# First loads of the query and key weights in row parts, two more homes for residual tiles, and a new instruction order in a fused adaLN attention and MLP block

## The chip, the cores and the metric

The kernel runs on one core of a Trainium2 chip. The metric is the device time of one execution in microseconds (us). Before the change three runs took 323.55, 323.23 and 323.64 us, a median of 323.55 us. A difference of 0.2% of that is 0.65 us.

## What is computed

One transformer block with adaptive layer norm, on 2048 tokens of width D = 640, all in bfloat16. The reference, cut to what matters:

```python
mod = (silu(c) @ w_mod)                      # 6 vectors of 640
sa, ca, ga, sb, cb, gb = mod                 # shift, scale, gate, twice
h = layernorm(x) * (1 + ca) + sa
q, k, v = split(h @ wqkv)                    # 32 heads of 20
scores = q @ k.T * 20 ** -0.5                # key j is seen by query i where 0 <= i - j < 256
x = x + ga * ((softmax(scores) @ v) @ wo)
h = layernorm(x) * (1 + cb) + sb
x = x + gb * ((sigmoid(h @ w_gate) * (h @ w_up)) @ w_down)   # hidden width 1536
```

## The kernel before

The tokens go through in 8 chunks of 256, two blocks of 128 each. A chunk `a` passes these stages: layer norm (`ln1`), the projections to Q, K and V (`qkv`), attention in two halves of 16 heads (`attention`), output projection and residual add (`outproj`), second layer norm, and the MLP (`mlp`). In attention the keys of one half are done in score sets, five a half (two for the first chunk, in three pieces): a set is a group of small matmuls into the one PSUM tile S, ScalarE (ACT) takes the exponentials of it into a tile E (line 1019), GpSimd (POOL) masks E (line 1044), and after the last set TensorE (PE) multiplies E with V in one burst. Because there is one S, PE cannot begin a set before ACT has read the set ahead of it.

The program is not run in the order in which it is written. Every operation is recorded in a list with its engines, a duration and its dependencies. `Prog.schedule` then walks the operations in the order of a table of numbers, `PRIO`: each entry gives an operation its rank (number divided by 5) and its engine (the remainder: 0 PE, 1 ACT, 2 VectorE = DVE, 3 POOL, 4 SyncE = SP). The scheduler also keeps a clock of estimates, with which the table was searched; the emitted program holds only the order, the choice of engine, the choice of buffers in each pool, and the semaphore waits. Each engine takes its instructions strictly in that order, so an instruction that waits holds up all that stands behind it on its engine. That holds for SP and ACT, which issue the DMAs, too.

What the change touches:

- `load_w3` (before: line 638) loads a column range of `wqkv` (640 x 1920, held as 128 partitions x 5 row tiles x 1920). Q's and K's columns come in four pieces of 320 columns, 400 KB each; V's in one piece of 800 KB. `R_w3` holds the resource that a projection waits for, one for each 160 columns.
- `qkv` (line 912) multiplies the normalized chunk `hT` with five row tiles of `wqkv`, a chain of five matmuls into one PSUM bank. For the first chunk a chain is 320 columns wide, later 480.
- `p_x1`, the pool of tiles that hold the residual x: 6 homes. The first three chunks' x stays in it from the start (`KEEP` = 3); later chunks load x again in `outproj` (line 1136), and that load waits for the stores of the chunk three earlier, which frees the home (`stored.get(a - 3)`).
- `load_x` (line 613), the loads of x, with estimates of how late they land.
- `mod_rows` makes two of the modulation vectors on PE from parts of `w_mod`, which lie for a time in the room of `wu` and of `hh`; matmuls written `M<-wu,silubc` and `M<-hh,silubc` are these.

Of the kernel before, what the change touches and what calls it, by code (L numbers as in the profile page):

```python
# [13 lines left out]
D = 640  # L14
# [3 lines left out]
NDT = D // 128  # L18
# [63 lines left out]
class Prog:  # L82
# [70 lines left out]
    def schedule(self):  # L153
# [37 lines left out]
        for o in sorted(self.ops, key=lambda x: x.prio):  # L191
# [41 lines left out]
            if o.isdma:  # L233
# [6 lines left out]
                o.end = max((own if e == "act" and own < bw else bw) - 0.83, st + dur)  # L240
                s = rr
# [120 lines left out]
def c_pe(n):  # L362
# [122 lines left out]
KEEP = 3  # L485
# [25 lines left out]
def build(nc, A_x, A_wqkv, A_wo, B_x, B_w_gate, B_w_up, B_w_down, c, w_mod, out, S=2048):  # L511
# [61 lines left out]
    def R(name):  # L573
        return Res(name)
# [716 lines left out]
```

## Time and profile before

| | |
|---|---|
| median of three runs | 323.55 us (323.23 to 323.64) |
| the profiled execution's own time | 324.34 us |
| its span, first to last instruction | 322.6 us |
| granted TensorE clock | 1.000 |
| PE busy | 316.8 us (98%), 4877 matmuls |
| ACT busy | 218.0 us (68%) |
| DVE busy | 207.1 us (64%) |
| POOL busy | 177.0 us (55%) |

A row of the profile names the line, the engine, the operation, the tile that is written and the tiles that are read, and the shape. Rows in order of time begin with the start and the length in us; what stands in brackets is the idle time of the engine ahead of the row and what ended it. PEld is the loading of weights into TensorE, which overlaps the matmuls. The chain that ended last is followed back from the last instruction, at each step to what released it. Matmuls are pipelined, so the length of a row of many matmuls reaches a little into the next row; the distance from start to start is the time that a row costs.

### The profile page before, as it was taken

To read this page: it belongs to the slowest core of one execution; us is meant where nothing else is said; L and a number is where in the kernel's file an instruction comes from. 1 tells how busy PE (TensorE), PEld (TensorE's weight loads), DVE (VectorE), ACT (ScalarE), POOL (GpSimd) and SP (SyncE) were. 2 spreads that over 40 slices of the span, in tenths; PEclk is the share of its full clock that TensorE was granted. 3 is DMA by queue.
4 is the path that set the end of the run, shared out by engine and by line. 5 is a ranking of instruction groups with operands and counts; after the bars stand their busy time and mean duration, and the time that the engine had idled before them with its cause. 6 is when DMAs were issued, how large, how long until landed. Compare 5 with 4: busy or idle time off the path is not lost.

```text
span 322.6 us, 11622 instructions
## 1 busy us (share of the span) xinstructions
PE 316.8 (98%) x4877; PEld 223.2 (69%) x4877; DVE 207.1 (64%) x420; ACT 218.0 (68%) x327; POOL 177.0 (55%) x268
## 2 busy tenths in 40 slices
PE   8899999999999999999999999999999999999996
PEld 3565545556876577767766667876887788887885
DVE  5688997886689658683756565637572765464232
ACT  2689888799887979688878686877767563110120
POOL 4237985978566675856566555666547366002000
PEclk9999999999999999999999999999999999999999
DMA  7979999799992753465024572530222031305101
GB/s 229 364 246 394 233 214 177 146 171 207 274 156 48 118 93 87 99 95 144 9 63 93 94 111 69 71 93 13 68 65 67 2 83 34 90 3 63 42 22 41
DMA packets 71182, 37.85 MB, mean 117 GB/s; under 512 B 45274, under 2 KB 69338, under 8 KB 71130
## 3 DMA queue, kind: packets, MB, share of 16 engines
q1 hardware_dynamic: 70112, 35.96, 50.2%
q10 hardware_dynamic: 1018, 1.15, 1.1%
q8 instruction: 38, 0.62, 0.8%
q14 instruction: 14, 0.11, 0.1%
HBM read 21.30 MB, written 5.25 MB: 82 GB/s over the span
## 4 chain that ended last, share of the span: by engine, by line
PE 92%; SPq 3%; DMA 2%; issue 1%; ACT 1%; DVE 0%; ACTq 0%
PE M L692 76%; PE S L693 8%; PE M L693 7%; SPq L588 3%; DMA wqkv<-in_A_wqkv_dram 2%; ACT E L1019 1%; DVE hh L1196 0%; ACT sig L1194 0%; DVE x L1215 0%; ACTq L335 0%
## 5 line engine op out<-in xcount | busy, mean ns | idle before, releaser
L1019 ACT ACTIVATE E<-S 128x512 bf16<-128x512 f32 (+2 forms) x184 | 150.4, 878 | 38.1 <-PE S L693 34.9
L1044 POOL TENSOR_SCALAR_AFFINE_SELECT E<-E 128x512 bf16<-128x512 bf16 (+1 forms) x176 | 139.3, 819 | 58.1 <-ACT E L1019 18.8
L692 PE MATMUL M<-wqkv,hT 128*128 128x480 bf16 (+1 forms) x340 | 73.0, 355 | 1.6 <-DMA wqkv<-in_A_wqkv_dram 1.6
L692 PE MATMUL M<-h2T,wu 128*128 128x256 bf16 x480 | 64.8, 273 | 0.0
L692 PE MATMUL M<-h2T,wg 128*128 128x256 bf16 x480 | 64.6, 273 | 0.0
L1196 DVE SCALAR_TENSOR_TENSOR hh<-sig,M 128x512 bf16<-128x512 f32 x48 | 32.5, 682 | 42.1 <-ACT sig L1194 28.4
L692 PE MATMUL M<-wd,hh 128*128 128x320 bf16 (+2 forms) x396 | 57.7, 295 | 0.1
L1194 ACT ACTIVATE sig<-M 128x512 f32<-128x512 f32 x48 | 28.9, 601 | 39.5 <-PE M L692 37.7
L692 PEld LDWEIGHTS M<-h2T,wg 128*128 128x128 bf16 x480 | 45.8, 98 | 8.1 <-issue 0.2
L692 PEld LDWEIGHTS M<-h2T,wu 128*128 128x128 bf16 x480 | 45.7, 98 | 7.5
L692 PEld LDWEIGHTS M<-wqkv,hT 128*128 128x128 bf16 x340 | 30.5, 98 | 28.0 <-DMA wqkv<-in_A_wqkv_dram 1.9
L692 PEld LDWEIGHTS M<-wd,hh 128*128 128x128 bf16 x396 | 37.4, 98 | 14.7 <-DVE hh L1196 0.3
L693 PEld LDWEIGHTS S<-QT,KT 20*64 20x64 bf16 (+1 forms) x1856 | 19.9, 100 | 19.4 <-ACT E L1019 8.1
L693 PE MATMUL S<-QT,KT 20*64 20x256 bf16 (+5 forms) x1856 | 32.1, 228 | 0.2 <-ACT E L1019 0.2
L1215 DVE TENSOR_TENSOR x<-M,x 128x320 bf16<-128x320 f32 (+2 forms) x33 | 15.7, 475 | 25.3 <-PE M L692 25.1
L778 DVE BATCH_NORM_STATS2 st<-x 128x6 f32<-128x320 bf16 x64 | 28.2, 477 | 2.2 <-DMA x<-in_A_x_dram 1.9
L1088 DVE STREAM_TRANSPOSE T<-M 128x512 f32<-128x512 f32 x32 | 21.6, 698 | 9.7 <-PE M L693 9.4
L692 PE MATMUL M<-wo,oT 128*128 128x320 bf16 x160 | 25.9, 300 | 0.1
L784 POOL TENSOR_SCALAR st<-st 128x2 f32<-128x2 f32 (+1 forms) x17 | 4.0, 235 | 37.0 <-DVE st L780 34.9
L693 PE MATMUL M<-E,V 128*32 128x128 bf16 (+1 forms) x960 | 22.8, 246 | 0.0
L693 PEld LDWEIGHTS M<-E,V 128*32 128x32 bf16 x960 | 19.0, 97 | 4.1 <-POOL E L1044 1.9
L1149 DVE TENSOR_TENSOR x<-M,x 128x320 bf16<-128x320 f32 x32 | 15.3, 482 | 8.9 <-PE M L692 8.6
(78 smaller groups left out, 237.1 us busy)
## 6 DMA issues: line engine op xcount, KB each, us to landing
x<-in_A_x_dram SPq DMA_DIRECT2D x23, 160.0 KB
doc<-On SPq DMA_DIRECT2D x64, 40.0 KB
wd<-in_B_w_down_dram SPq DMA_DIRECT2D x4, 480.0 KB
out_dram<-x SPq DMA_DIRECT2D x11, 160.0 KB
wqkv<-in_A_wqkv_dram SPq DMA_DIRECT2D x4, 400.0 KB
wu<-in_w_mod_dram SPq DMA_DIRECT2D x5, 320.0 KB
oT<-doc SPq DMA_DIRECT2D x8, 192.0 KB
wd<-in_w_mod_dram SPq DMA_DIRECT2D x4, 320.0 KB
```

What stands on the lines that cost most here:

```text
L588: return e.dma_start(dst(), src())
L692: return e.matmul(o, l, r, start=st, stop=sp, skip_group_check=True)
L693: return e.matmul(o, l, r, start=st, stop=sp, tile_position=tp, skip_group_check=True)
L778: A("dve", lambda e, g, bi=bi, j=j: e.bn_stats(v(bi * 12 + j * 6, 6), src[bi].ap[:, j * 320:(j + 1) * 320]), 0.48, reads=[src[bi].r()], wr ...
L784: A("pool", lambda e, g, lo=lo, hi=hi: e.tensor_scalar(v(28 + lo, hi - lo), var()[:, lo:hi], EPS, None, op0=ALU.add), 0.2, reads=[st.r(("m ...
L1019: A("act", lambda e, eng: e.activation(dst(), src(), ACT.Exp, scale=SM_SCALE), c_act(n), reads=[Sp.r()], writes=[E.r(key)], prio=3, tag=f" ...
L1044: A("pool", lambda e, eng: e.affine_select(rows(dst), rows(src), pattern=[[0, 8], [sign, n]], compare_op=ALU.is_ge, fill=0.0, base=base, c ...
L1088: A("dve", lambda e, g, h=h: e.transpose(T1.ap[:, 512 * h:512 * h + 512], X[h].ap), 0.694, reads=[X[h].r()], writes=[T1.r(h)], prio=3.5, t ...
L1149: A("dve", lambda e, g, ps=ps, bi=bi, half=half: e.tensor_tensor(x1[bi].ap[:, half * 320:half * 320 + 320], ps.ap[:, 0:320], x1[bi].ap[:, ...
L1194: A("act", lambda e, g, pg=pg, sg=sg: e.activation(sg.ap[:], pg.ap[:], ACT.Tanh, scale=0.5), c_act(512), reads=[pg.r()], writes=[sg.r()], ...
L1196: A("dve", lambda e, g, pu=pu, sg=sg, f0=f0: e.scalar_tensor_tensor(out=hh.ap[:, f0:f0 + 2, :], in0=sg.ap[:].rearrange("p (a b) -> p a b", ...
L1215: A("dve", lambda e, g, ps=ps, bi=bi, c0=c0, n=n: e.tensor_tensor(x1[bi].ap[:, c0:c0 + n], ps.ap[:, 0:n], x1[bi].ap[:, c0:c0 + n], op=ALU. ...
```

## The change

Four pieces of code change, and the whole table `PRIO` is another one. The pieces of Q's first 320 and K's first 320 columns are loaded in two DMAs each, of two and of three row tiles, and a projection waits for the part that its row tile lies in. The pool `x1` has 8 homes in place of 6, and the reload of a chunk's x waits for the stores of the chunk four earlier. The scheduler's estimates of landing times grow: of `wqkv` (0.6 to 1.2 us, and V's from the default to 1.2 us), of x blocks 2 and 3, and of all loads whose estimated landing lies between 15.3 and 36.0 us, by 1.1 us. These estimates are used only in the search of the order and change no wait in the program. Matmuls and their shapes are the same in number.

```diff
@@ Prog.schedule
                 o.end = max((own if e == "act" and own < bw else bw) - 0.83, st + dur)
+                if 15.3 < o.end < 36.0 and not turn:
+                    o.end += 1.1
@@ the table, all entries
 PRIO = [
-    118, 123, 218, 113, 73, 693, 288, 513, 1493, 93, 503, 67, 258, 332, 302, 743, 126, 4, 29, 39, 44, 49, 54, 59, 34,
...
@@ build
-    p_x1 = sbpool("x1", 6, [128, D])
+    p_x1 = sbpool("x1", 8, [128, D])
...
-    R_w3 = [R(f"wqkv{i}") for i in range(12)]
+    R_w3 = [[R(f"wqkv{i}a"), R(f"wqkv{i}b")] for i in range(12)]
...
-    def load_w3(lo, hi, work, prio, tag, **kw):
-        dma(lambda: wqkv[:, :, lo:hi], lambda: wqkv_src[:, :, lo:hi], work, writes=R_w3[lo // 160:hi // 160], prio=prio, tag=tag, **kw)
+    def load_w3(lo, hi, work, prio, tag, parts=((0, NDT),), **kw):
+        for t0, t1 in parts:
+            dma(lambda t0=t0, t1=t1: wqkv[:, t0:t1, lo:hi], lambda t0=t0, t1=t1: wqkv_src[:, t0:t1, lo:hi], work * (t1 - t0) / NDT,
+                writes=[r for rs in R_w3[lo // 160:hi // 160] for r, t in zip(rs, (0, 2)) if t0 <= t < t1], prio=prio, tag=tag, **kw)
...
-        load_w3(320 * i, 320 * i + 320, 1.05, 0.30 + 0.005 * i, "wq" if i < 2 else "wk", lat=0.6)
+        load_w3(320 * i, 320 * i + 320, 1.05, 0.30 + 0.005 * i, "wq" if i < 2 else "wk", parts=((0, 2), (2, NDT)) if i in (0, 2) else ((0, NDT),), lat=1.2)
...
-    load_w3(2 * D, 3 * D, 2.1, 0.34, "wv")
+    load_w3(2 * D, 3 * D, 2.1, 0.34, "wv", lat=1.2)
@@ qkv
-            pe_chain(ps, wid, pairs, [R_w3[lo // 160:hi // 160] + [hT[a].r((kt, bi))] for kt in range(NDT)], prio, f"proj{name}{a}", hold=hold, first=a == 0 and hi <= 2 * D)
+            pe_chain(ps, wid, pairs, [[rs[kt >= 2] for rs in R_w3[lo // 160:hi // 160]] + [hT[a].r((kt, bi))] for kt in range(NDT)], prio, f"proj{name}{a}", hold=hold, first=a == 0 and hi <= 2 * D)
@@ outproj
-            x1 = [load_x(p_x1, 2 * a + bi, 15, eng=XE, extra=stored.get(a - 3, ())) for bi in range(2)]
+            x1 = [load_x(p_x1, 2 * a + bi, 15, eng=XE, extra=stored.get(a - 4, ())) for bi in range(2)]
```

What the new table does to the order is shown at three places. Names in these rows carry buffer numbers where they help: x10 to x17 are homes of the pool x1, x00 to x03 of the pool x0.

**SP, the first loads of weights and x.** Before, from the end of the loads of `w_mod` (its last two are 128x640 into wd) on:

```order
L588 DMA wd<-in_w_mod_dram 128x640 x2
L588 DMA wqkv<-in_A_wqkv_dram 128x5x320 x2
L588 DMA x12<-in_A_x_dram 128x640
L588 DMA x13<-in_A_x_dram 128x640
L588 DMA wqkv<-in_A_wqkv_dram 128x5x320
L588 DMA wqkv<-in_A_wqkv_dram 128x5x640
L588 DMA x14<-in_A_x_dram 128x640
L588 DMA wqkv<-in_A_wqkv_dram 128x5x320
L588 DMA x15<-in_A_x_dram 128x640
```

The same place in the change:

```order
L591 DMA wd<-in_w_mod_dram 128x640 x2
L591 DMA wqkv<-in_A_wqkv_dram 128x2x320
L591 DMA wqkv<-in_A_wqkv_dram 128x3x320
L591 DMA wqkv<-in_A_wqkv_dram 128x2x320
L591 DMA x12<-in_A_x_dram 128x640
L591 DMA wqkv<-in_A_wqkv_dram 128x3x320
L591 DMA x13<-in_A_x_dram 128x640
L591 DMA wqkv<-in_A_wqkv_dram 128x5x320
L591 DMA wqkv<-in_A_wqkv_dram 128x5x640
L591 DMA wqkv<-in_A_wqkv_dram 128x5x320
L591 DMA x14<-in_A_x_dram 128x640
L591 DMA x15<-in_A_x_dram 128x640
```

Two pieces have become four parts, and x14 has moved from ahead of the last piece of `wqkv` to behind it.

**PE, the wait for that last piece.** The rows carry the semaphores that they wait for; `sem_d16` is the last piece's before. Before:

```order
L693 MATMUL S0<-QT0,KT0 128x256 [waits sem_act]
L693 MATMUL S0<-QT0,KT0 128x256 x7
L692 MATMUL M<-ident,x03 128x128 [waits sem_dve]
L692 MATMUL M<-ident,x02 128x128
L692 MATMUL M<-ident,x03 128x128 [waits sem_dve]
L692 MATMUL M<-ident,x02 128x128
L692 MATMUL M<-ident,x03 128x128 [waits sem_act]
L692 MATMUL M<-ident,x02 128x128
L692 MATMUL M<-wqkv,hT0 128x320 [waits sem_dve,sem_d16]
L692 MATMUL M<-wqkv,hT0 128x320 x4
```

In the change the last piece's semaphore is `sem_d17`:

```order
L698 MATMUL S0<-QT0,KT0 128x256 [waits sem_act]
L698 MATMUL S0<-QT0,KT0 128x256 x7
L697 MATMUL M<-ident,x03 128x128 [waits sem_dve]
L697 MATMUL M<-ident,x02 128x128
L697 MATMUL M<-ident,stg 128x128 [waits sem_dve]
L697 MATMUL M<-ident,stg 128x128 x3
L697 MATMUL M<-wqkv,hT0 128x320 [waits sem_act,sem_d17]
L697 MATMUL M<-wqkv,hT0 128x320 x4
```

Counted from the first projection, PE has 24 of these 128-wide transposing matmuls before the wait in the old order and 28 in the new one; the 35 projection matmuls and the two score sets before it are as many.

**PE, the second half-chunk's edge set** (the score set of 32 small matmuls 128x64) and the main set that follows it (24 matmuls 64 wide or more). `M<-hh,silubc` is the second of the two modulation products. Before:

```order
L693 MATMUL S<-QT,KT 128x64 x32
L692 MATMUL M<-wqkv,hT 128x480 x5
L692 MATMUL M<-ident,stg 128x128 x8
L692 MATMUL M<-wqkv,hT 128x480 x2
L693 MATMUL S<-QT,KT 64x256 x8
L693 MATMUL S<-QT,KT 64x192 x8
L693 MATMUL S<-QT,KT 64x64 x8
L692 MATMUL M<-wqkv,hT 128x480 x10
```

In the change:

```order
L698 MATMUL S<-QT,KT 128x64 x32
L697 MATMUL M<-ident,stg 128x128 x8
L697 MATMUL M<-wqkv,hT 128x480 x5
L698 MATMUL M<-hh,silubc 32x320 x20
L698 MATMUL S<-QT,KT 64x256 x8
L698 MATMUL S<-QT,KT 64x192 x8
L698 MATMUL S<-QT,KT 64x64 x8
L697 MATMUL M<-wqkv,hT 128x480 x10
```

The modulation product stood behind two main sets and the ten projection matmuls between them; now it stands ahead of the first of these sets. On SP the last part of what it reads, the second load of 128x2x1280 from `w_mod` into hh, now stands behind the four stores of the first attention half (`doc0<-On0`), while before it stood one load and two transposes ahead of the first of them.

Beyond these, ACT issues 7 of the 128x640 stores of x and 5 of the 128x640 loads of x in the change, against 4 and 3 before; SP issues 8 and 21, against 11 and 23 before. Of the modulations of h2T, ACT has 16 (24 before), DVE 11 (5), POOL 13 (11).

More of the change, by code (lines that the diff above doesn't have):

```diff
@@ L615, in load_x @@
         dma(lambda: t.ap[:], lambda: x_flat[b * 128:(b + 1) * 128, :], 0.5 if b < 2 else 0.47 if b < 8 and (pool is p_x0 or b < 2 * KEEP) else 0.6, writes=[t.r()], prio=prio, tmin=tmin,
-            tag=f"x{b}" if pool is p_x0 or b < 2 * KEEP else f"y{b}", eng=eng, lat=0.2 + DSAFE + (1.2 if 4 <= b < 16 and pool is p_x0 or 4 <= b < 2 * KEEP else 0.0), extra=extra)
+            tag=f"x{b}" if pool is p_x0 or b < 2 * KEEP else f"y{b}", eng=eng, lat=0.2 + DSAFE + (1.2 if 4 <= b < 16 and pool is p_x0 or 4 <= b < 2 * KEEP else 0.7 if b in (2, 3) and pool is p_x1 else 0.0), extra=extra)
         return t
```

224 rows, old and new, of the table PRIO are left out of this document.

## Prediction

> **What bounds the kernel now.** I read the head of the page first, then the waits of PE, then the chain of work that ended last, then PE's rows in order of time at the places where the chain leaves PE. The page and the waits of PE (engine, line, what it waited for: us in total, times, longest):
>
> ```profile
> span 322.6 us, 11622 instructions
> PE 316.8 (98%) x4877; PEld 223.2 (69%) x4877; DVE 207.1 (64%) x420; ACT 218.0 (68%) x327; POOL 177.0 (55%) x268
> ...
> PE M L692 <- DMA wqkv<-in_A_wqkv_dram: 1.6, 2, 0.8
> ...
> PE S L693 <- ACT E L1019: 0.2, 1, 0.2
> ```
>
> PE is busy for 98% of the span, and of all its waits that the view counts, two for `wqkv` make 1.6 us and one for an exponential 0.2 us. The number and shapes of the matmuls do not change. So this is a kernel at the speed of its matmuls, and the change can gain only what stands in these rows and in gaps of a tenth or two elsewhere; it can lose more, where a new order opens a wait. The tail offers nothing either: the chain's last rows are matmuls without a gap and one residual add.
>
> ```profile
> 299.99 20.20 PE M L692 x182
> 320.20 0.02 issue
> 320.22 0.29 DVE x L1215
> ```
>
> The start of the chain (start, us, what) and PE's rows there:
>
> ```profile
> 10.14 1.07 SPq L588
> 11.21 0.04 issue
> 11.25 8.00 DMA wqkv<-in_A_wqkv_dram
> 19.25 0.05 issue
> 19.30 1.87 PE M L692 x16
> ...
> 10.97 2.40 PE L692 MATMUL M<-wqkv,hT 128*128 128x320 bf16 x15 [0.81 <-DMA wqkv<-in_A_wqkv_dram]
> 15.78 1.52 PE L692 MATMUL M<-wqkv,hT 128*128 128x320 bf16 x10
> 17.14 0.28 PE L692 MATMUL M<-ident,x 128*128 128x128 bf16 x2
> 17.25 0.43 PE L692 MATMUL M<-wqkv,hT 128*128 128x320 bf16 x2
> 17.66 0.40 PE L693 MATMUL S<-QT,KT 20*128 20x256 bf16 x8
> 17.99 0.51 PE L692 MATMUL M<-ident,x 128*128 128x128 bf16 x6
> 19.30 1.53 PE L692 MATMUL M<-wqkv,hT 128*128 128x320 bf16 x10 [0.80 <-DMA wqkv<-in_A_wqkv_dram]
> ```
>
> From start to start, ten 320-wide matmuls cost 17.14 - 15.78 = 1.36 us, 0.136 each, and a 128-wide one (17.25 - 17.14) / 2 = 0.055. The six at 17.99 are through at 18.32, and PE stands until 19.30: 0.98 us, for the last piece of `wqkv`, issued at 11.25 and landed 8.00 us later. Why so late? The windows view (stretch; busy time and count of PE, PEld, DVE, ACT, POOL; clock, DMA share, GB/s) and the DMA view of 16 to 20 us, in forty slices of 0.1 us:
>
> ```profile
> 12.00:14.00 2.00, 2.00 (x20) 1.33 (x20) 1.74 (x5) 1.69 (x5) 0.71 (x5) 1.00 1.09 381
> 16.00:17.00 1.00, 1.00 (x9) 0.70 (x8) 1.00 (x4) 1.00 (x2) 0.58 (x3) 1.00 1.17 386
> 17.00:18.00 1.00, 1.00 (x16) 0.44 (x14) 1.00 (x3) 0.88 (x2) 0.49 (x1) 1.00 0.65 239
> 18.00:19.00 1.00, 0.50 (x10) 0.32 (x6) 0.97 (x3) 1.00 (x2) 0.00 (x0) 1.00 0.15 45
> ...
> GB/s 390 352 391 371 346 416 416 352 503 320 365 339 307 301 269 179 154 179 154 141 109 90 58 38 32 38 13 26 26 26 13 38 26 26 64 128 243 218 282 256
> q8 instruction: 1, 0.02, 1.7%
> ```
>
> The 16 DMA engines move 381 to 386 GB/s until 17, some 24 each. From about 18.3 to 19.3 the core moves 13 to 38 GB/s: the share of one engine. One instruction fetch (q8) falls into this stretch; I read it as having put that engine behind, and the last piece waits for it.
>
> **The change, part by part.** The sum is made as a difference to the profiled execution's 324.34 us and carried to the median of 323.55, which lies 0.79 us lower.
>
> *The last piece of `wqkv`.* In the new order x14 (128 x 640 in two bytes, 160 KB, 0.164 MB) goes behind it. At 386 GB/s that is 0.42 us, so with the same laggard the piece lands at 19.25 - 0.42 = 18.83. PE has four more 128-wide matmuls to do first, 0.22 us, and arrives at 18.54. What stood at 19.30 + 0.22 = 19.52 in the old order then starts at about 18.83: a gain of **0.69**. If the laggard misses the piece, PE is the later one and the gain is 19.52 - 18.54 = 0.98. If the two additional DMAs each held the queue for an issue of 2.33 / 5 = 0.47 us (the row of five loads below), the piece would come 0.94 later, at 19.77, a loss of 0.25. I take 0.69, from the same place and the same bytes.
>
> ```profile
> 2.17 2.33 SPq L588 DMA_DIRECT2D wd<-in_w_mod_dram  x5
> ```
>
> At this point a page speaks against the parts. The Trainium skill, "DMA: Bandwidth & Descriptors", section "Anatomy of one DMA — SWDGE (gpsimd) path", gives every DMA a fixed 2.0 us beside its bytes, measured on another engine's path. If two more such costs stood in a row ahead of the last piece, it would land 4.0 us later and the time would be some 3.2 us over the one before, 326.7, instead of below it. The rows disagree: 381 GB/s between 12 and 14 us is a full queue of loads of 0.16 to 0.8 MB, and a 0.41 MB piece with 2.0 us of its own would move at 0.41 / (2.0 + 1.1) = 0.13 MB a us.
>
> *The first parts.* PE's first projection waited 0.81 us until 10.97 for a whole piece of 400 KB; a first part is 160 KB, so it is there some 0.6 us sooner (0.246 MB at 381 GB/s). But the loads between are no fewer, and PE meets the last piece's landing in any case: whatever is won here is waited for there. I take 0; it is worth up to 0.3 if the last piece comes early, and below nothing only by the issues above.
>
> *The second modulation product* now stands between the edge set and the main set behind it. Before:
>
> ```profile
> 41.53 1.19 PE L692 MATMUL M<-wqkv,hT 128*128 128x480 bf16 x5
> 43.00 0.57 PE L692 MATMUL M<-wqkv,hT 128*128 128x480 bf16 x2
> 43.80 0.43 PE L693 MATMUL S<-QT,KT 20*64 20x256 bf16 x24 [0.23 <-ACT E L1019]
> 46.68 0.86 PE L693 MATMUL M<-hh,silubc 128*32 128x320 bf16 x20
> 47.48 1.79 PE L692 MATMUL M<-wqkv,hT 128*128 128x480 bf16 x8
> ...
> 41.68 2.06 ACT L1019 ACTIVATE E<-S 128x512 bf16<-128x512 f32 x4 [0.22 <-PE S L693]
> ```
>
> The four exponentials take 2.06 us, and PE has seven 480-wide and eight small matmuls for them, then waits 0.23. In the new order it gives up two 480-wide matmuls here (0.41) and does the product (47.48 - 46.68 = 0.80): 0.39 more, which covers the wait. Gain **0.23**. Its cover must be there: the product needs its last load, which now is issued behind four stores of the first attention half.
>
> ```profile
> 32.41 1.25 DVE L1097 STREAM_TRANSPOSE On<-Tn 128x1024 bf16<-128x1024 bf16 x1
> 37.18 1.21 SPq L588 DMA_DIRECT2D doc<-On  x3
> 35.00:40.00 5.00, 5.00 (x123) 3.09 (x121) 4.57 (x11) 4.15 (x7) 4.88 (x9) 1.00 1.08 286
> 0.79 0.39 SPq L588 DMA_DIRECT2D x<-in_A_x_dram  x1
> 3.12 0.89 DVE L778 BATCH_NORM_STATS2 st<-x 128x6 f32<-128x320 bf16 x2 [1.67 <-DMA x<-in_A_x_dram]
> ```
>
> The stores' source is ready at 33.66; four stores at 0.40 put the load's issue at 35.3. With little ahead of it, it lands after 2.33 us (the first load of x) and 1.7 more for 480 KB more at 286 GB/s, at 39.4; behind a queue as full as the start's, after 8.00, at 43.3. PE wants it at about 42.4 (the wait's 43.8 less the two matmuls' 0.41, the 0.23 and the 0.69). By the nearer rows there are 3 us in hand; at the far end 0.9 is lost. I take 0.
>
> *Turns between forms of matmul* (score set, burst, all else): counted in the order they go from 170 to 172. The two matmuls at 17.25 should be through at 17.52 and the set starts at 17.66, so a turn costs up to 0.14; I take 0.05 each, a loss of **0.10**, with 0 and 0.28 as ends.
>
> *The two homes, and moves between engines.* An earlier reload of x gains only if someone waits for it.
>
> ```profile
> DVE x L1149 <- PE M L692: 8.6, 15, 1.5
> DVE x L1215 <- PE M L692: 25.1, 18, 2.6
> 132.52 0.35 ACTq L588 DMA_DIRECT2D out_dram<-x  x1
> ```
>
> The residual adds wait for PE, and no row has them wait for x: 0. ACT gets five more DMA issues at 0.35, but eight modulations fewer; 0, with the case below for what an issue may wait for.
>
> *All other places* of a new order: before, gaps of 0.2 to 0.3 are what I find between 20 and 320 us; I let as many come as go, 0, with 0.3 gained and 1.5 lost as ends.
>
> Sum: -0.69 - 0.23 + 0.10 = **-0.82**, 323.52 for a profiled execution like the one before, 322.7 for the median.
>
> **The rivals.** *The gain is given back to ACT.* There is one S, and ACT is busy for most of the next 20 us; if ACT sets the pace, PE's earlier start ends in longer waits at score sets. For it: the wait of 0.23 at 43.80. Against it: it is the only one of PE's that the view counts. The 0.69 is lost, and 323.55 - 0.13 = 323.4 is left.
>
> *The parts do not do what they say,* because each DMA holds the queue: the last piece at 19.77, a loss of 0.25 in place of 0.69 gained, 323.55 + 0.25 - 0.13 = 323.7. The Trainium skill's fixed cost would be the extreme of it, at 326.7; the 381 GB/s leave that 1 in 100, counted with the slow case.
>
> *ACT's additional stores hold it up* (slower). A store waits in ACT's order for a residual add; exponentials and sigmoids stand behind it. Adds wait up to 2.6 us for PE (row above), and at a set without spare cover, as at 43.80, ACT's delay becomes PE's. One such place costs up to about 2 us, so 323.55 - 0.82 + 2.0 = 324.7; it decides for slower from 1.5 us on. For it: four more such places. Against: the stores on ACT before, as at 132.52, show no idle ACT ahead of them.
>
> **How the numbers follow.** Forecast 50 in 100, given back 22, parts useless 10, ACT held up or a new wait like it 18. The forecast's own range runs from 321.9 (0.98 for the last piece, 0.3 for the first parts, 0.23, 0.1 elsewhere) to 323.2. A measurement of this kernel tells 0.2%, 0.65 us, from no change, so the forecast's last tenth counts as no change: faster 0.47, same 0.34, slower 0.19. The range for 8 in 10 reaches from 321.9 to 324.5, over the two middle cases and half of the slow one.
>
> **What would show it.** Right: PE's wait for the last piece falls from 0.98 to about 0.3 with the ten matmuls behind it starting near 18.8; no wait ahead of the main set after the edge set; the matmuls from there to the end as dense as before. Wrong: the last piece lands after 19.3; a wait of PE for the hh load near 42; ACT idle ahead of a store while PE waits for an exponential; any new row among PE's waits over 0.3 us.

## The result and the profile after

Eleven runs of the change gave a median of 325.95 us (323.69 to 326.55), eleven of the kernel before 323.64 us (323.23 to 324.20). The ratio is **1.0061, 95% interval 1.0043 to 1.0080**: the change is slower by 0.6%, some 2 us. The forecast was 322.7 us, 0.26% faster, with a range of 321.9 to 324.5.

The execution whose profile came with this result shows nothing of that. The head of its page, and the waits of PE (engine, line, what it waited for: us in total, times, longest):

```profile
span 321.9 us, 11617 instructions
...
PE S L677 <- DVE E L672: 1.3, 1, 1.3
PE M L697 <- DVE hT L853: 1.2, 1, 1.2
PE S L697 <- DMA wd<-in_w_mod_dram: 0.2, 1, 0.2
```

Its span is 0.7 us shorter than before's 322.6, both waits for `wqkv` are gone, and so is the one for an exponential. PE's rows at the places of the forecast (start, length, what):

```profile
9.80 0.31 PE L697 MATMUL S<-silubc,wd 128*128 128x64 bf16 x5
11.33 2.56 PE L697 MATMUL M<-wqkv,hT 128*128 128x320 bf16 x16 [1.22 <-DVE hT L853]
...
18.93 1.52 PE L697 MATMUL M<-wqkv,hT 128*128 128x320 bf16 x10
...
42.67 0.86 PE L698 MATMUL M<-hh,silubc 128*32 128x320 bf16 x20
43.47 0.43 PE L698 MATMUL S<-QT,KT 20*64 20x256 bf16 x24
...
54.97 0.41 PE L698 MATMUL S<-QT,KT 20*128 20x64 bf16 x32
55.32 1.53 PE L697 MATMUL M<-wo,oT 128*128 128x320 bf16 x10
```

The ten matmuls behind the last piece start at 18.93 (19.30 before); PE comes to them there without a wait, the last completion of the piece being in at 18.41. The second modulation product runs at 42.67 without a wait, and the score set behind it starts at once. This execution took 323.69 us, the shortest of the eleven. So the question was what the other ten do.

### The profile page after: what moved, and what is told of

Its sections match the earlier page's. It is cut to its first block, busy times and chain, and to the rows that moved or that the text cites. A ratio compares the mean times of both kernels' runs of the same rounds, so it can differ in the third digit from the quotient of the medians.

```text
span 321.9 us, 11617 instructions
## 1 busy us (share of the span) xinstructions
PE 316.5 (98%) x4877; PEld 223.0 (69%) x4877; DVE 207.3 (64%) x423; ACT 216.4 (67%) x324; POOL 177.0 (55%) x268
## 4 chain that ended last, share of the span: by engine, by line
PE 96%; DMA 2%; SPq 1%; DVE 0%; issue 0%; DVEq 0%
PE M L697 80%; PE S L698 8%; PE M L698 7%; DMA wd<-in_w_mod_dram 2%; SPq L591 1%; PE S L697 0%; PE S L687 0%; DVE hT L853 0%; DVE x L1220 0%; DVE mA L769 0%; DVEq L337 0%
## 5 line engine op out<-in xcount | busy, mean ns | idle before, releaser
L697 PE MATMUL M<-h2T,wu 128*128 128x256 bf16 x480 | 65.9, 273 | 0.0
L698 PEld LDWEIGHTS S<-QT,KT 20*64 20x64 bf16 (+1 forms) x1856 | 19.9, 101 | 19.3 <-ACT E L1024 8.4
L783 DVE BATCH_NORM_STATS2 st<-x 128x6 f32<-128x320 bf16 x64 | 29.0, 477 | 2.3 <-DMA x<-in_A_x_dram 1.8
L698 PEld LDWEIGHTS M<-E,V 128*32 128x32 bf16 x960 | 19.1, 97 | 4.5 <-POOL E L1049 2.1
```

The lines of the kernel that those rows point to most:

```text
L697: return e.matmul(o, l, r, start=st, stop=sp, skip_group_check=True)
L698: return e.matmul(o, l, r, start=st, stop=sp, tile_position=tp, skip_group_check=True)
L783: A("dve", lambda e, g, bi=bi, j=j: e.bn_stats(v(bi * 12 + j * 6, 6), src[bi].ap[:, j * 320:(j + 1) * 320]), 0.48, reads=[src[bi].r()], wr ...
```

## The experiments

Most were made with an order table rewritten, the change's or that of before: an operation or a stretch of the order is moved, and the rest keeps its order and engines. Where code differs too, the edit shows it. Each median stands beside runs of the kernel before on the same chip. The ratio is to those; it is taken over all runs of both, and differs from the quotient of the two medians by up to 0.002. r1 to r4 ran on one chip, r5 to r12 on a second, r13 to r16 on a third, r17 and r18 on a fourth.

### A usual execution of the change, and its halves

The change once more (r1_again, no edit):

> The changed kernel once more, to see an execution of it of the usual length (its median is 325.95 us, while the profiled one took 323.69). Theory A (a landing at the start): about 326, and PE has one wait of 1.5 to 2.5 us for a load before 45 us that the first profile does not have; from 45 us to the end the rows stand as far apart as there. Theory B (ACT's DMA issues later on): about 326, PE is at 60 us where it is in the first profile, within 0.3 us, and loses about 2 us behind it, in several waits for exponentials.

325.9 us, ratio 1.0058 (1.0034 to 1.0081). Its profiled execution took 325.78 us. PE's waits:

```profile
span 324.0 us, 11617 instructions
...
PE M L697 <- DMA oT<-doc: 1.3, 1, 1.3
PE S L677 <- DVE E L672: 1.3, 1, 1.3
PE M L697 <- DVE hT L853: 1.2, 1, 1.2
PE S L697 <- DMA wd<-in_w_mod_dram: 0.4, 1, 0.4
```

and its rows at the same places:

```profile
10.55 0.31 PE L697 MATMUL S<-silubc,wd 128*128 128x64 bf16 x5
12.09 2.56 PE L697 MATMUL M<-wqkv,hT 128*128 128x320 bf16 x16 [1.22 <-DVE hT L853]
...
19.69 1.52 PE L697 MATMUL M<-wqkv,hT 128*128 128x320 bf16 x10
...
55.77 0.41 PE L698 MATMUL S<-QT,KT 20*128 20x64 bf16 x32
57.49 1.52 PE L697 MATMUL M<-wo,oT 128*128 128x320 bf16 x10 [1.31 <-DMA oT<-doc]
```

Two differences make up the 2.1 us between the two spans. The last product of the first modulation comes 0.75 us later (10.55 for 9.80), and the ten matmuls are later by the same (19.69 for 18.93 is 0.76). Then PE waits 1.31 us for `oT`, the output of attention read back for the projection `wo`; the set ahead of it is 0.80 later, `wo` 2.17. Behind that the rows stand as far apart as in the first profile: the last matmul is 2.09 later. Theory A, a landing at the start, had the right kind of wait but not the place (it is at 56 us, not before 45); theory B (ACT's stores) falls.

Two kernels try the code and the order apart. In r2_whole the first pieces are loaded whole, in the change's order:

```diff
-        load_w3(..., parts=((0, 2), (2, NDT)) if i in (0, 2) else ((0, NDT),), lat=1.2)
+        load_w3(..., lat=1.2)
```

> The changed kernel with the first pieces of wqkv loaded whole, all else and the order of all else as in the change. If the parts themselves cost the time (two more DMAs, smaller ones): 323.5 or below, 2 us under the change. If the order does, by A or by B: within 0.5 us of the change, 325.5 to 326.4.

325.02 us, 1.0031 (1.0016 to 1.0045): between the two expectations. The profiled execution, the shortest of its twelve, has no wait for `oT`. r3_oldorder has parts, 8 homes and waits of the change in the old order:

```diff
-PRIO = [ the change's ]
+PRIO = [ before's, each second part with its first part's rank ]
```

> All code of the change (parts, 8 homes), but the order and the engines of before; the second part of a piece is issued right behind the first. If the parts themselves cost the time: 325.5 to 326.4. If the new order does, by A or by B: 323.4 to 324.0, like before.

324.26 us, 1.0013 (0.9998 to 1.0027). So the new order is what costs; whether the parts cost something was left to r14. r4_newhead keeps the change's first 461 entries, to about 60 us, and before's order behind them:

> The change's order up to about 60 us, and from there the order and the engines of before for all that is left. Theory A (a landing at the start): 325.5 to 326.5, as slow as the change. Theory B (ACT's DMA issues behind 60 us): 322.7 to 323.5, the gains of the start without the loss.

325.8 us, 1.0053 (1.0034 to 1.0071), with a wait of 0.9 us for `oT` in its profile, and one of 1.7 us for the first rows of `w_mod`. The loss lies in the first 60 us.

### The wait for oT: SP's order and the landing

SP's rows in r1_again (start; length of the issue):

```profile
42.10 2.29 SPq L811 DMA_TRANSPOSE KT<-stg  x1
44.48 0.52 SPq L591 DMA_DIRECT2D x<-in_A_x_dram  x1
45.10 1.86 SPq L811 DMA_TRANSPOSE QT<-stg  x1
47.05 1.63 SPq L591 DMA_DIRECT2D doc<-On  x4
48.77 0.35 SPq L591 DMA_DIRECT2D gbc<-gate  x1
49.17 1.55 SPq L591 DMA_DIRECT2D wu<-in_B_w_up_dram  x1
50.85 1.25 SPq L811 DMA_TRANSPOSE KT<-stg  x1
52.14 0.56 SPq L590 DMA_DIRECT2D gate<-gq  x1
53.29 0.39 SPq L591 DMA_DIRECT2D oT<-doc  x1
```

SP is never idle for 0.2 us until the last row (0.59 ahead of that), and the load of `oT` is issued at 53.29. In the first profile of the change the same rows end with:

```profile
48.00 0.43 SPq L591 DMA_DIRECT2D wu<-in_B_w_up_dram  x1
...
51.22 0.40 SPq L591 DMA_DIRECT2D oT<-doc  x1
```

There the load is issued 2.07 us earlier, while PE is only 0.8 earlier: the transposing DMA into KT at 42.1 took 1.27 us to issue in place of 2.29, the load into `wu` 0.43 in place of 1.55. A second execution of the kernel before (r5_before) shows the old order:

> The kernel before once more, to see a second execution of it, above all its start and the second load of oT. Theory A2 (two waits of the change that the first profile happened not to have): the second load of oT lands at least 1 us ahead of PE's first wo matmul; and where the first products of the modulation come later than in the first profile (6.18 us), PE still starts the ten matmuls behind the last piece of wqkv within 0.3 us of 19.30, because its wait for that piece gives the time back. Rival (any order loses as much in a usual execution): a wait for oT here too, or the ten matmuls as much later as the products.

324.08 us, 0.9984 (0.9968 to 1.0001) against further runs of itself. SP there:

```profile
42.05 1.26 SPq L806 DMA_TRANSPOSE KT<-stg  x1
43.38 2.06 SPq L806 DMA_TRANSPOSE QT<-stg  x1
...
47.10 1.17 SPq L588 DMA_DIRECT2D doc<-On  x3
48.38 1.24 SPq L806 DMA_TRANSPOSE KT<-stg  x1
49.72 2.00 SPq L806 DMA_TRANSPOSE QT<-stg  x1
51.89 0.47 SPq L588 DMA_DIRECT2D oT<-doc  x1
```

The load of `oT` is issued at 51.89, its last completion is in at 55.79, and PE comes to it at 56.95: 1.16 us in hand. In r1_again PE comes at 56.12 (the set at 55.77 and the 0.35 that it costs), 0.83 sooner, the issue is 1.40 later, and the last completion is in at 57.36: 1.24 us short. PE comes sooner because of its own order: in the old one ten projection matmuls, 2.04 us (54.91 to 56.95 in r5_before), stand between that set and `wo`, and in the new one they stand behind `wo`. In the stretch of SP from 42 us to this load QT0 has gone behind it and the first load of `oT` ahead of the stretch, and the load of x02, a load into `wu` and the write of the second gate row have come in; the issues add up to 10.0 us in place of 9.0. And it is one DMA engine that opens the wait: 15 of the 16 completions of r1_again's load are in by 55.97. With the 1.2 us of before such a laggard costs little; without them PE waits for it.

One edit to the change moves the load of `oT` up (r6_oT_early), as order rows of SP:

```diff
 DMA gbc<-gate1
-DMA wu<-in_B_w_up_dram
 DMA_TRANSPOSE KT3<-stg
+DMA oT0<-doc0
+DMA wu<-in_B_w_up_dram
 DMA gate3<-gq
-DMA oT0<-doc0
```

> The change with one move on SP: the second load of oT stands behind the transposing DMA into KT3, ahead of the load into wu and the write of the second gate row, which follow it. Theory A2: the wait of PE for oT near 56 us (1.3 us in the second execution of the change) is gone, 324.6 (324.2 to 325.0). Rival (the queue as a whole is late, and the wait only moves to the next load or transpose): 325.5 or more, with a new wait of PE over 0.5 us between 45 and 65 us.

325.18 us, 1.0031 (1.0009 to 1.0053). In its profile the load is issued at 51.87, complete at 54.39, and the wait is gone: `wo` starts at 56.16 where r1_again, with its products at the same time, has 57.49. The median is 0.7 under r1_again's, on another chip, and over the 324.2 to 325.0 expected. With the old start as well, r7_oldstart shows what an earlier start is worth while `oT` is late:

```diff
-order: the change's
+order: before's first 112 entries (about 14 us), then the change's
```

> The change with the order of before for the first 112 entries (about the first 14 us: modulation products, first modulations of hT, loads of wqkv and x, with x14 ahead of the last piece again), and the change's order behind them. Theory A2: the first projection follows the last product by 1.0 us in place of 1.4, and the time is 0.3 to 0.8 under the change, 325.1 to 325.6, with the wait for oT still there. Rival (the start costs nothing, all of it is oT): 325.7 to 326.1.

325.12 us, 1.0016 (0.9995 to 1.0036). In the profiled execution the start was quick, the ten matmuls at 18.09, and PE stood all the longer:

```profile
54.26 0.41 PE L698 MATMUL S<-QT,KT 20*128 20x64 bf16 x32
56.86 1.52 PE L697 MATMUL M<-wo,oT 128*128 128x320 bf16 x10 [2.19 <-DMA oT<-doc]
```

The set is 1.51 us earlier than in r1_again, and `wo` only 0.63: the earlier start is mostly waited away. But here SP is not late. The load is issued at 51.45, earlier than in r5_before, and takes 5.27 us to its last completion (3.90 in r5_before). The chain of that stretch has

```profile
51.45 5.27 DMA oT<-doc
```

From 54.3 to 56.3 us all DMA queues of the core together move 15 GB/s. So neither the issue nor a queue at full rate accounts for the last 2 us of this landing; what does is open. Both edits together (r8_both):

> Both edits together: the order of before for the first 112 entries, and the second load of oT moved up on SP. Theory A2: both terms add, 323.6 to 324.3, about the kernel before. Rival (the waits move on): 325.2 or more.

325.0 us, 1.0017 (0.9996 to 1.0038): a miss for A2 by the median, since only five of its twelve runs lie below 324.5. Its profile has a wait of 0.5 us for QT at 58.6. The rival was right in this: the wait moved to the next transposing DMA. So r11_relief takes more out of SP's way:

```diff
 (r8_both, order rows of SP)
-DMA x02<-in_A_x_dram                 (ahead of the four stores doc0<-On1)
 DMA oT0<-doc0
+DMA x02<-in_A_x_dram
-DMA wu<-in_B_w_up_dram
-DMA gate3<-gq
 DMA_TRANSPOSE QT0<-stg
 DMA_TRANSPOSE KT2<-stg
+DMA wu<-in_B_w_up_dram
+DMA gate3<-gq
```

> The order of before for the first 112 entries, the second load of oT moved up, and three more DMAs taken out of SP's way between 43 and 54 us: the load of x02 behind the load of oT, the load into wu and the write of the second gate row behind the transposing DMA into KT2. Theory A2 with SP as the bound between 42 and 58 us: neither a wait for oT nor one for QT, 323.3 to 324.2, at or under before. Rival (what is late is the DMA engines, not their issue): 324.8 to 325.3 as with the move of oT alone, with a wait of PE over 0.4 us between 50 and 65 us.

324.03 us beside 324.08 for before, ratio 1.0012 (0.9991 to 1.0033). Its profile, with a span of 322.2 us, has only the two waits of the start:

```profile
PE S L677 <- DVE E L672: 1.3, 1, 1.3
PE M L697 <- DVE hT L853: 0.8, 1, 0.8
```

By the median SP's theory holds, but the moves change two things at once. In the twenty profiled executions the load of `oT` takes 2.4 to 2.7 us from its issue to its last completion in the eight kernels that have it ahead of the load into `wu` (r6, r8 and r10 to r15), and 3.3 to 5.3 us in the other twelve. So the moves shorten the landing as well as bring the issue forward, and no run here separates the rival (the DMA engines are late, not their issue) from the queue of SP.

### The start: a wait that was cover

Two kernels start later, by four idle matmuls ahead of the last products:

```diff
-FILL = (2, 2, 2, 0, 0)
+FILL = (2, 2, 2, 4, 0)
```

In the kernel before (r9_before_late):

> The kernel before with four more idle matmuls of 512 columns (0.86 us of PE, writing nothing that is read) ahead of the last products of the modulation, so that the first projection comes 0.86 us later. Theory A2 (the wait for the last piece of wqkv is cover for a late start): PE starts the ten matmuls behind that piece at 19.3 to 19.8, and the time is 0 to 0.4 over before. Rival (a late start costs what it is late): the ten matmuls 0.86 later, at 20.1, and the time 0.8 to 0.9 over before.

In r6_oT_early's order (r10_oT_early_late):

> The change with the second load of oT moved up on SP, as in an earlier run (325.2, 1.003 times before), and with the same four idle matmuls ahead of the last products. Theory A2 (the change has no cover left at the start): the ten matmuls stand as far behind the last product as without the four, 9.0 us, and the time is 0.7 to 0.9 over that run, 1.005 to 1.006 times before. Rival (it is covered here too): within 0.3 of that run, 1.002 to 1.004 times before.

PE in r9_before_late, and then in r10_oT_early_late:

```profile
9.60 1.03 PE L682 MATMUL S<-E 128*128 128x512 bf16 x4
...
11.97 2.44 PE L692 MATMUL M<-wqkv,hT 128*128 128x320 bf16 x15 [0.78 <-DVE hT L848]
...
19.47 1.52 PE L692 MATMUL M<-wqkv,hT 128*128 128x320 bf16 x10
...
50.72 0.56 PE L692 MATMUL M<-wqkv,hT 128*128 128x480 bf16 x2 [1.55 <-DMA KT<-stg]
```

```profile
12.94 2.56 PE L697 MATMUL M<-wqkv,hT 128*128 128x320 bf16 x16 [1.22 <-DVE hT L853]
...
20.54 1.52 PE L697 MATMUL M<-wqkv,hT 128*128 128x320 bf16 x10
```

Starts of three rows in every execution that tells of this (the last products of the modulation from the same rows):

| execution | last product | first projection | ten matmuls | last piece in |
|---|---|---|---|---|
| before | 9.96 | 10.97 | 19.30 | 19.25 |
| r5_before | 10.23 | 11.20 | 19.23 | 19.18 |
| r9_before_late | 11.00 | 11.97 | 19.47 | 18.03 |
| change | 9.92 | 11.33 | 18.93 | 18.41 |
| r1_again | 10.67 | 12.09 | 19.69 | 19.14 |
| r10_oT_early_late | 11.53 | 12.94 | 20.54 | 17.74 |

(A product's time is here that of its last small matmul; the last column is the last of the sixteen completions of the last piece.) In the old order 1.04 us of lateness, from the first to the third row, leave 0.17 at the ten matmuls: what PE loses ahead of the first projection it no longer waits for the last piece. In the change 1.61 us of lateness arrive as 1.61.

Whether there is a wait at all depends on the execution too. In before and r5_before fifteen of the sixteen completions are in by 17.87 and 17.95, and the last comes 1.2 to 1.4 us behind them. In r9_before_late it does not, and PE's own path, 7.50 us from the first projection to the ten matmuls, sets the 19.47. Of the nine profiled executions that load x14 ahead of the piece only three (before, r5_before, r15_relief_whole) make PE wait for it; of the eleven with x14 behind it none does.

The first projection follows the last product by 1.41 to 1.42 us in place of 0.97 (1.01 in the first profile, where it waits for `wqkv`): in the old order it waits for the first modulation that DVE makes of hT, in the new one for the third, and eight of them take 1.87 us, 0.23 each. With the piece in time the ten matmuls stand 9.01 us behind the last product in the change and 8.47 in the old order (r9_before_late): by these rows the new start costs 0.54 us.

By the times the two runs are less clear. r9_before_late: 325.0 us, 1.0029 (1.0001 to 1.0056), but six of its twelve runs lie at 323.8 to 324.8, like before, and the others reach 327.8. The profiled one is of the long ones (326.9) and has the wait of 1.55 us for KT in the fence above; that the other long ones have it too is a reading. In SP's rows the load into `wg` and that into `wu` ahead of it took 2.46 and 1.99 us to issue, where r5_before has 1.02 and 0.40; the transposing DMA into KT is issued 2.64 us later than there, and takes 5.89 us to its last completion in place of 4.06. So the old order has little to spare there either. r10_oT_early_late: 325.34 us, 1.0045 (1.0028 to 1.0062), 0.16 us over r6_oT_early by the median where 0.7 to 0.9 were expected, and 0.0014 more by the ratio; the marks of its profile are 0.9 later at 20 us and 1.0 later at the end. The mechanism is shown by the rows, its price not by the times.

### How the loss divides, and where the gains go

> The order of before for the first 112 entries, the second load of oT moved up, and the first pieces of wqkv loaded whole again. If the parts themselves cost time: 0.5 to 0.9 under the same kernel with parts (325.0, 1.0017 times before), that is 0.999 to 1.000 times before. If not: within 0.3 us of it.

r12_whole_both gave 323.98 us, 1.0018 (0.9996 to 1.0041): 1.0 us under r8_both by the median, and not under it by the ratio (1.0017). Of the next four r13_relief_only is r11_relief with the change's own start, r14_relief_only_whole that with whole pieces, r15_relief_whole is r11_relief with whole pieces (edits as above), and r16_change is the change.

> The change's own order at the start, with the four moves on SP (the second load of oT up; the load of x02, the load into wu and the write of the second gate row behind it). What is open is how the loss divides. If SP's part is 1.3 us and the start's 0.4 to 0.9: 324.4 to 324.9, 1.2 to 1.5 under the change on the same chip and 0.4 to 0.9 over the kernel with the old start and the same moves (324.0). If the start costs nothing once SP is relieved: 323.8 to 324.2.

> The same with the first pieces of wqkv loaded whole. If the parts cost time by themselves (two earlier pairs of kernels had the one with whole pieces 0.9 and 1.0 under the other): 0.6 to 1.0 under the kernel with parts. If those pairs differed by what waits happened to open: within 0.3 of it.

> Old order for the first 112 entries, the four moves on SP and whole first pieces: all that lost time taken out of the change, and what gained left in (the second modulation product ahead of the main set, the order behind it, 8 homes). If the parts cost time: 323.0 to 323.4, 0.6 to 1.0 under the kernel with parts (324.0) and 0.2 to 0.3% under before. If not: 323.7 to 324.1, like before.

> The change as it is, on the same chip as the three runs above, for the differences to it and for a third execution's trace: 325.5 to 326.2, with the wait of PE for oT near 56 us of 0.8 to 2.2 us.

| run | median us | ratio to before (95%) |
|---|---|---|
| r16_change | 325.91 | 1.0059 (1.0038 to 1.0081) |
| r13_relief_only | 325.00 | 1.0036 (1.0021 to 1.0051) |
| r14_relief_only_whole | 325.03 | 1.0036 (1.0021 to 1.0051) |
| r15_relief_whole | 325.04 | 1.0036 (1.0015 to 1.0057) |

r13 against r16: the moves on SP are worth 0.9 us, though the intervals overlap. What the start is worth in time is not settled: r13 against r11 (another chip) gives 0.0024 of the time, 0.8 us; r6 against r8, on one chip, 0.0014; and r14 against r15, on one chip, nothing. r14 against r13: the parts cost nothing that these runs can tell; that the two earlier pairs (r2, r12) differed by which waits had opened is a reading. r15 missed both its expectations: in its profile the wait for the last piece is back at 0.67 us, and PE waits 0.7 us for QT at 65.4. r16's profile has no wait for `oT`, against what I expected; it has 1.3 us for the first row of `w_mod` and 0.5 for QT at 59.5. **Which** of SP's transposes and loads is late changes from execution to execution; that one of them between 45 and 66 us is, is the rule: of the twelve profiled executions that have the change's order from 14 us on, the one of the result left out, eight have a wait for `oT` or QT there, of 0.5 to 2.2 us.

The last two kernels make the two gaining moves in the kernel before. r17_x14:

```diff
 (order rows of SP)
 DMA wqkv<-in_A_wqkv_dram 128x5x640
-DMA x14<-in_A_x_dram 128x640
 DMA wqkv<-in_A_wqkv_dram 128x5x320
+DMA x14<-in_A_x_dram 128x640
```

> The kernel before with one move: x14 is loaded behind the last piece of wqkv, as in the change; whole pieces, 6 homes, old order otherwise. It tries the largest term of the forecast alone. Forecast's term: the ten matmuls behind the last piece start 0.3 to 0.5 sooner, at 18.7 to 19.0, and the time is 0.3 to 0.5 under before, 0.9985 to 0.999. Rival (what PE gains there it waits for at the next DMA of SP, a KT, QT or oT between 36 and 65 us): the ten matmuls at 18.7 to 19.0, but the time within 0.2 of before or over it.

324.45 us beside 324.08, 1.0017 (1.0000 to 1.0034). r18_x14_hh has also, in the order rows of PE,

```diff
+MATMUL M<-hh,silubc x20
 MATMUL S<-QT,KT x24
 MATMUL M<-wqkv,hT x10
 MATMUL S<-QT,KT x24
-MATMUL M<-hh,silubc x20
```

> The same, and the second modulation product stands ahead of the main set behind the edge set, as in the change; its loads stay where they were. Forecast's term: the wait of 0.39 us ahead of that set is gone and the time is 0.2 to 0.4 under the run with x14 alone, 0.9975 to 0.998 times before. Rival (the set, 0.4 later, makes ACT and the burst behind it later by as much, or SP's DMAs do): within 0.2 of that run or over it, with a new wait of PE of 0.3 to 0.6 between 45 and 60 us.

324.44 us, 1.0016 (0.9997 to 1.0034). Both intervals exclude what the forecast's terms had given (0.9985 to 0.999, 0.9975 to 0.998), so the rivals hold by the times. In r17 the ten matmuls start at 18.89, 0.34 before r5's 19.23; that is PE's own arrival, 7.51 us behind the first projection, the piece being in at 17.82. The lead is still there at 78 us, later than the rival had named; in this execution it ends here (PE, then the chain of that stretch):

```profile
18.89 1.38 PE L692 MATMUL M<-wqkv,hT 128*128 128x320 bf16 x9
...
84.85 0.84 PE L693 MATMUL M<-E,V 128*32 128x128 bf16 x32 [0.27 <-POOL E L1044]
```

```profile
74.84 6.41 DMA hT<-x
...
81.84 0.58 ACT sig L1194
...
83.70 1.10 POOL E L1044
...
84.85 1.16 PE M L693 x45
```

A transposing DMA lands 6.41 us after its issue, ACT is late by it, POOL masks late, and PE's burst waits. In r18 the wait of 0.39 at 43 us is gone, and given back at the second set behind it, where the old order had the product as cover, and at the burst:

```profile
43.06 0.86 PE L693 MATMUL M<-hh,silubc 128*32 128x320 bf16 x20
43.86 0.43 PE L693 MATMUL S<-QT,KT 20*64 20x256 bf16 x24
...
48.91 0.43 PE L693 MATMUL S<-QT,KT 20*64 20x256 bf16 x24 [0.37 <-ACT E L1019]
...
50.68 1.50 PE L693 MATMUL M<-E,V 128*32 128x128 bf16 x64 [0.23 <-POOL E L1044]
```

The change has ten projection matmuls (2.20 us) ahead of that set where r18 has eight, and no wait there; so r18 prices the move alone.

No kernel tried here is faster than before beyond its interval.

## Why the prediction was wrong

- **What bounds the kernel.** That PE does is right. (The view also counts 1.3 us for E at the start, which the list left out; every execution here has it.) Wrong was to read the 0.98 us ahead of the last piece as time lost in each execution. It is what is left when the first products come early and one completion of the piece comes late; otherwise it is smaller (0.64 us in r5_before, 0.11 in r9_before_late, from the end of the six matmuls ahead). As the piece is long in with those 0.11, they are no wait, and the 0.98 was some 0.1 too large by itself.
- **The last piece of `wqkv`, 0.69.** That PE does not wait for it with x14 behind it is right in all eleven executions. That the ten matmuls then start at 18.93 in the change's first profile, for a forecast of 18.8, is luck: the forecast has the landing there, and it is PE's arrival, with the piece in at 18.41. The landing itself was taken from one execution; its last completion lies between 17.4 and 19.1 us with x14 behind the piece and between 17.5 and 19.4 with x14 ahead. The step that failed is "PE has four more 128-wide matmuls to do first, 0.22 us, and arrives at 18.54". It took all of PE's path from one execution of the old order. In the new order the first projection stands 0.45 later behind the last product, PE arrives at 18.93 to 20.54 (three rows of the table), and nothing is left to absorb a late product. The row that the forecast had moved from 19.52 to 18.83 stands at 19.69 in a usual execution: 0.17 lost in place of 0.69 gained.
- **The first parts, 0.** Nothing speaks against it by itself (r14 against r13). I looked at DMA only, and not at which of DVE's modulations the first matmul of the new order waits for: 0.45 us.
- **The second modulation product, 0.23.** At its place the gain came, and the loads of hh were in time in every execution: the 3 us in hand were rightly read. In r18, without the rest of the new order, it was given back within 8 us. In the change itself the stretch from 40 to 50 us has 0.26 us less beyond the matmuls' own time in r1_again than in r5_before.
- **Turns, 0.10.** From 19 to 30 us r1_again has 0.25 us more of such time than r5_before, without a wait that the view counts; whether turns make it was not tried.
- **Homes and moves between engines, 0.** No store and no reload of x on ACT is among what any of these executions waits for; r3_oldorder bounds homes, parts and waits together at 0 to 0.9 us.
- **All other places, 0.** This is the term that failed most: 1.3 us (0 to 2.2) for `oT` or a transpose of QT. In part it could have been worked out from the order: ahead of the load of `oT` SP's rows issue for 8.3 of 9.4 us already in the profile of before (9.0 of 9.8 in r5_before), the load has 1.7 us in hand there (1.2), and the new order takes 2.04 us of matmuls from ahead of PE's first product with it and puts more DMAs ahead of the load. How long it takes to land (2.4 to 5.3 us) could not. I followed the load of hh past SP's other work, and no other.
- **The rivals.** The slow case had the right sign and nearly the size (324.7), but named ACT's stores where it is a load and a transposing DMA on SP. "Given back to ACT" is what became of the two gaining moves alone in the profiled executions (r17, r18), beginning in r17 with a transposing DMA.

Put together, an estimate from the starts of the matmuls in the traces of r1_again (325.78 us) and r5_before (324.11), by time beyond what the matmuls of a stretch cost where nothing waits (where a stretch is cut moves each figure by up to 0.2): 0.20 lost to 19.3 us, 0.25 to 30, 0.31 gained to 50, 1.40 lost to 60, 0.03 gained behind that, 1.51 of the 1.67 between them.

What stays open: why the first rows of `w_mod` let the products begin anywhere from 5.5 to 7.5 us, what stretches a DMA's issue on SP and its landing, which of these two makes the load of `oT` late, and the exact shares of start and SP, whose intervals overlap.

## What to carry to other kernels

Before a wait is priced as a gain, ask what it absorbs: if the row ahead of it can come late in another execution, the wait is cover, and a second profile or a few idle matmuls put in on purpose tell. In a reordered program follow every load that the bounding engine waits for through the queue of the engine that issues it, with the longest issue time that the trace shows for each row ahead of it, and on to its last completion. A profile is one execution; where its time is at an end of the spread of the timed runs, take another.

## What was unexpected of the hardware

The issue of one and the same DMA on SP takes very different times: a transposing DMA of 128 x 8 x 128 from 1.23 to 2.64 us within r1_again and up to 2.87 in r9_before_late, a load of 128x2x768 into `wu` 0.43 or 1.55 us (r1_again's and the first profile's rows above). The Trainium skill, "Perfetto Trace Analysis", section "DMA Instruction — HWDGE (DVE, Sync)", says that the interval of such a row covers the taking of the descriptor generator and the generating, not the movement of the data. That it varies does not speak against this; the page gives no figure, and that a full queue stretches it is not shown here.

One DMA engine of 16 can run 1.4 us behind the others, and a wait that is for all of them takes that price: the last completion of r1_again's load of `oT` is at 57.36, the one ahead of it at 55.97, while in r6_oT_early all lie between 53.93 and 54.39. An instruction fetch falls into r1_again's stretch, as one did at the last piece of `wqkv` before; that it is the cause is a reading, and a fetch alone does not do it: r12_whole_both has one at 16.8 us, as before has, and its last piece has the last completion 0.28 us behind the fifteenth, where before has 1.38.
